# An mLSTM with two mixtures of dense layers: state in one 64x64 plane, gates partly on GpSimd, a lag between two blocks, and a new order

## The chip, the cores and the metric

The kernel runs on one core of a Trainium2 chip. The metric is the device time of one execution in microseconds (us). The engines of the core are named as the profile names them: PE is TensorE (matmuls; PEld is its weight load), DVE is VectorE, ACT is ScalarE, POOL is GpSimd, SP issues all the DMAs. POOL works on SBUF alone, PE writes PSUM alone, and PSUM has eight banks of 512 fp32 columns here.

## The reference

Three layers follow each other. The first is a recurrent one: 2 batches of 8 heads, 768 steps, head size 40. The other two are dense layers over the 1536 tokens.

```python
for t in range(S):                       # per head: state C (40x40), n (40), m
    m_new = max(f[t] + m, i[t]);  f_s = exp(f[t] + m - m_new);  i_s = exp(i[t] - m_new)
    C = f_s * C + i_s * outer(v[t], k[t]);   n = f_s * n + i_s * k[t]
    y[t] = sigmoid(o[t]) * (C @ q[t]) / max(abs(n @ q[t]), 1)
h = y @ w_in;  g = P(h) / (Q(abs(h)) + 1e-6);  x = g @ w_out        # 320 -> 2048 -> 320
xn = x / rms(x) * rms_g;  out = (silu(xn @ w_gate) * (xn @ w_val)) @ w_out2   # 320 -> 1536 -> 320
```

## The kernel before

**Stages.** The recurrent layer is cut into 12 chunks of 128 steps (6 for each batch, numbered j). In a chunk the steps are done as matrix products: `s` (keys times queries, L504), `f` (forget gates spread over the partitions, L484), `scan` (their running products, L487), `a` (product of the two, L509), `y` (times the values, L537). What earlier chunks left comes from the state tile `cst`: `yi` multiplies it with the queries (L527), `ys` scales that and takes it out of PSUM (L531), and `u` (L549), `cd` (L555) and `ca` (L563, L565) bring the state up to date. Then come the denominator, the output gate and a transpose (`xt`, L645) into `xall`.

The first dense layer works on pairs (block of 256 tokens, 256 of the 2048 columns): 48 pairs, each with 16 matmuls in (L676), a chain of some ten elementwise operations on ACT, DVE and POOL (L709 to L749), and matmuls out (L681, or L695 and L697). `PAIRS` lists them: blocks 0 and 1 in turn over the eight column groups, then blocks 2 to 5. The weights arrive as 64-bit words that DVE, ACT and POOL turn into fp32 halves (`weight`, L304 to L392). The second dense layer (L846 to L960) has its matmuls at L865 and L873 to L875.

**The gates.** One tile holds the gates of all 16 heads on 16 partitions. They are worked in two parts, steps 0 to 255 and 256 to 767: running maximum (L423), sums (L430, L431 on DVE, L434 on POOL), exponential (L437), forget factors in fp16 (L441), running products in a chunk (`gate_d`, L449), transposes (L455). No chunk can start its `f` before L441 of its part.

**The state.** `cst` is 128 partitions by 4 pairs of heads by 2 by 41. Even heads stand on partitions 0 to 39 in plane 0, odd heads on 64 to 103 in plane 1, and the rest is kept zero, so that one matmul over 128 partitions gives both heads of a pair. POOL clears that rest once (L409, L410).

**What sets the order.** Nothing is scheduled on the chip or by the compiler: every step is a task, `ORDER` is a list of 1948 task numbers, and each engine gets its instructions in the sequence in which the tasks stand there. Tiles and PSUM banks are taken from rings (`ring("b", banks)` for the eight banks) when a task starts and given back when another ends, so the list also decides which bank each task writes and what it has to wait for. `yi` takes one bank (L615), `ys` gives it back.

Of the kernel before, what the change touches and what calls it, by code (L numbers as in the profile page):

```python
# [121 lines left out]
def kernel(  # L122
# [148 lines left out]
    for nm, n in (("k", 2), ("v", 2)):
        ring("l" + nm, tiles(at, n, [128, H, D], FP32, "l" + nm))
    qk_bufs = tiles(at, 2, [128, 2, HP, L], FP32, "lqk")
    ring("lqk", qk_bufs)
# [827 lines left out]
```

## Time and profile before

| | us |
|---|---|
| median of 3 runs (481.05 to 481.11) | 481.09 |
| the profiled execution's own time | 481.12 |
| its span, first to last instruction | 479.3 |
| PE busy | 456.4 |
| DVE busy | 331.1 |
| POOL busy | 317.5 |
| ACT busy | 304.8 |

The profile is of one execution. Its span is 1.8 us shorter than its time, which is what lies around the first and the last instruction. Busy times are shares of the span: PE has hardly a gap, the three elementwise engines are about two thirds busy, but in stretches: the 40 slices of the page show DVE at 8 or more from the second slice to the 25th, and ACT from the fifth, with one 7, to the 24th.

### The profile page before, as it was taken

How to read it: one execution, taken by the hardware profiler on the slowest of the kernel's cores; microseconds unless marked ns; L12 is line 12 of the kernel's file. 1: busy time of each engine (PE TensorE's matmuls, PEld its weight loads, DVE VectorE, ACT ScalarE, POOL GpSimd, SP SyncE). 2: the span in 40 equal slices, each digit the busy share in tenths (PEclk: the TensorE clock that was granted, in tenths of full speed). 3: DMA queues.
4: the chain of work that ended last, by engine and by line, in shares of the span. 5: the costliest groups of instructions: out<-in, count | busy, mean ns of one | idle time of the engine just before them, and what ended most of it. 6: DMA issues, size and time to landing. Idle time of an engine off the chain costs nothing.

```text
span 479.3 us, 9356 instructions
## 1 busy us (share of the span) xinstructions
PE 456.4 (95%) x3552; PEld 414.5 (86%) x3552; DVE 331.1 (69%) x609; ACT 304.8 (64%) x576; POOL 317.5 (66%) x337
## 2 busy tenths in 40 slices
PE   3699899989999999999999999999999999999996
PEld 2588778778789999999999988888898889999996
DVE  7999999999999989899999999875210210201211
ACT  3245999999998899799999988552422212212311
POOL 5689999999998898886977778990831303213320
PEclk9998999999999999999999999999999999999999
DMA  8869371325032060010322144571100000000001
GB/s 239 273 204 255 101 196 31 114 61 143 1 102 63 1 203 3 1 42 2 115 90 83 38 160 166 180 233 59 34 15 27 1 0 2 1 27 29 1 14 57
DMA packets 18366, 40.41 MB, mean 84 GB/s; under 512 B 3952, under 2 KB 11904, under 8 KB 18320
## 3 DMA queue, kind: packets, MB, share of 16 engines
q1 hardware_dynamic: 18320, 39.80, 27.4%
q8 instruction: 28, 0.46, 0.4%
q14 instruction: 18, 0.15, 0.1%
HBM read 35.86 MB, written 3.93 MB: 83 GB/s over the span
## 4 chain that ended last, share of the span: by engine, by line
PE 65%; ACT 14%; POOL 9%; DVE 8%; issue 3%; DMA 1%; POOLq 0%; DVEq 0%; ACTq 0%
PE bank L865 26%; PE bank L676 10%; PE bank L695 5%; PE bank L875 4%; PE bank L873 4%; PE bank L874 4%; PE bank L681 4%; POOL z L720 2%; PE bank L697 2%; ACT z L710 2%; ACT u L709 2%; ACT bank L732 2%; ACT vv L718 1%; DVE w_buf L487 1%; POOL cv L356 1%
## 5 line engine op out<-in xcount | busy, mean ns | idle before, releaser
L676 PE MATMUL bank<-xall,win 128*128 128x256 f32 x768 | 104.0, 289 | 3.5 <-ACT yb L543 1.6
L676 PEld LDWEIGHTS bank<-xall,win 128*128 128x128 f32 x768 | 96.5, 193 | 7.1 <-ACT yb L543 1.8
L941 DVE TENSOR_TENSOR vv<-bank,vv 128x512 f32<-128x512 f32 x35 | 23.6, 688 | 98.0 <-PE bank L865 97.8
L720 POOL TENSOR_TENSOR z<-z,u 128x512 f32<-128x512 f32 x48 | 62.0, 1292 | 14.1 <-ACT z L710 13.1
L947 POOL TENSOR_TENSOR wou<-vv,wou 128x512 fp32r<-128x512 f32 x16 | 20.7, 1295 | 53.7 <-ACT wou L944 49.4
L938 ACT ACTIVATE vv<-bank 128x512 f32<-128x512 f32 x35 | 20.7, 595 | 50.6 <-PE bank L865 46.2
L865 PE MATMUL bank<-xall,w2gv 128*128 128x512 f32 (+1 forms) x256 | 46.4, 337 | 0.0
L749 POOL TENSOR_TENSOR gl<-vv,gh 128x512 fp32r<-128x512 f32 x32 | 41.3, 1296 | 5.6 <-ACT gh L748 3.8
L865 PEld LDWEIGHTS bank<-xall,w2gv 128*128 128x128 f32 x256 | 39.2, 190 | 4.7 <-DVE vv L739 0.2
L710 ACT ACTIVATE z<-u,few 128x512 f32<-128x512 f32 x48 | 39.2, 816 | 1.0
L695 PE MATMUL bank<-wou,gh 128*128 128x320 f32 x128 | 38.9, 316 | 0.0
L697 PE MATMUL bank<-wou,gh 128*128 128x320 f32 x128 | 38.0, 309 | 0.0
L681 PE MATMUL bank<-scr,vv 128*128 128x320 f32 x128 | 37.1, 435 | 0.0
L737 DVE SCALAR_TENSOR_TENSOR bank<-vv,few,bank 128x512 f32<-128x512 f32 x48 | 35.8, 749 | 0.0
L735 DVE SCALAR_TENSOR_TENSOR z<-z,bank 128x512 f32<-128x512 f32 x48 | 32.6, 682 | 4.4 <-ACT bank L734 3.6
L732 ACT ACTIVATE bank<-z,few 128x512 f32<-128x512 f32 x48 | 32.9, 686 | 2.5 <-DVE vv L729 2.5
L739 DVE SCALAR_TENSOR_TENSOR vv<-z,bank 128x512 f32<-128x512 f32 x48 | 32.6, 683 | 0.6
L331 DVE TENSOR_SCALAR bank<-raw 128x320 int32<-128x320 int32 x68 | 32.6, 486 | 0.3
L709 ACT ACTIVATE u<-bank 128x512 f32<-128x512 f32 x48 | 28.7, 598 | 4.0 <-POOL z L720 1.8
L865 PE MATMUL bank<-win,w2gv 128*128 128x512 f32 x128 | 31.1, 391 | 0.0
L681 PEld LDWEIGHTS bank<-scr,vv 128*128 128x128 f32 x128 | 23.2, 190 | 8.2 <-DVE vv L739 0.2
L364 POOL TENSOR_TENSOR win<-cv,win 64x128 fp32r<-64x128 f32 (+2 forms) x37 | 28.0, 757 | 2.4 <-ACT win L360 0.5
(169 smaller groups left out, 1180.3 us busy)
## 6 DMA issues: line engine op xcount, KB each, us to landing
raw<-in_w_out_dram SPq DMA_DIRECT2D x14, 640.0 KB, 4.1
raw<-in_w_gv_dram SPq DMA_DIRECT2D x12, 640.0 KB, 4.3
raw<-in_w_in_dram SPq DMA_DIRECT2D x8, 640.0 KB, 5.8
lqk<-in_qk_tr_dram SPq DMA_DIRECT2D x24, 192.0 KB, 4.7
los<-in_o_gate_dram SPq DMA_DIRECT2D x12, 160.0 KB, 3.6
lv<-in_v_dram SPq DMA_DIRECT2D x12, 160.0 KB, 4.3
lk<-in_k_dram SPq DMA_DIRECT2D x12, 160.0 KB, 3.8
z_dram<-rnd SPq DMA_DIRECT2D x6, 320.0 KB, 4.8
```

Of the source, the lines that this page charges most:

```text
L331: DVE.tensor_scalar(out=mid(x), in0=word(x, 1), scalar1=3, scalar2=0x3FFFFFFF, op0=ALU.logical_shift_left, op1=ALU.bitwise_and,)
L676: PE.matmul(out=hb()[:, e], lhsT=l, rhs=r, start=(x == 0), stop=(x == len(mm) - 1))
L681: PE.matmul(out=T("acc", n, t)[:, 0:DM], lhsT=T("vv", i)[:, e, t * 128:(t + 1) * 128], rhs=w[:, e], start=p + e == 0, stop=p == NPAIR - 1 ...
L695: PE.matmul(out=o, lhsT=l, rhs=woh[:, e], start=first, stop=last)
L697: PE.matmul(out=o, lhsT=l, rhs=wol[:, e], start=False, stop=False)
L709: go("hu", lambda: ACT.activation(out=u(), in_=hb(), func=ACTF.Abs), [("in1", i)], ["u"])
L710: go("z", lambda: ACT.activation(out=z(), in_=u(), func=ACTF.Identity, scale=babs[:, 1:2], bias=babs[:, 0:1]), [("hu", i)], ["z"])
L720: go("zu", lambda: POOL.tensor_tensor(out=z(), in0=z(), in1=u(), op=ALU.mult), [("z", i)], [], ["u"])
L732: go("ars", lambda: ACT.activation(out=hb(), in_=z(), func=ACTF.Abs_reciprocal_sqrt, bias=cq), [("zu", i), ("p3", i)])
L737: go("y2", lambda: DVE.scalar_tensor_tensor(out=hb(), in0=vv(), scalar=nacoef[:, 0:1], in1=hb(), op0=ALU.add, op1=ALU.mult), [("w", i)])
L749: go("gl", lambda: POOL.tensor_tensor(out=gl(), in0=vv(), in1=r32(gh()), op=ALU.subtract), [("gh", i)], ["gl"], ["vv"])
L865: PE.matmul(out=bank(i, e), lhsT=l, rhs=r, start=y == 0, stop=y == len(mm) - 1)
```

## The change

Five edits, and a new order.

- The state loses its planes: `cst` is 128 by 4 by 41, odd heads stand below even ones in one plane. `yi` therefore multiplies each head by itself, in tiles of 64 partitions by 64 columns (16 calls of 41 columns in place of 8 of 82), and writes even and odd heads to two banks; `ys` becomes two operations of 164 columns. `cd` and `ca` become one operation each over all 128 partitions instead of two over 40.
- `u` loads 64 columns of keys instead of 40 (the next head's first 24 come along) and so writes all 128 partitions; the key tiles get 24 columns of zeros at their end (L411 of the changed kernel). The memsets of `lqk` and `cst` go.
- The three sums of the gates all run on one engine: DVE for the first part, POOL for the second.
- The running products of the gates take their zero from a word of a PSUM bank, where it was an SBUF tile.
- `LAG = 1`: the pairs of block 1 run one column group behind those of block 0.
- `ORDER` is another list throughout.

```diff
-    PAIRS = [(n, p) for p in range(NPAIR) for n in range(2)] + [(n, p) for n in range(2, NB) for p in range(NPAIR)]
+    PAIRS = [(n, x - n * LAG) for x in range(NPAIR + LAG) for n in range(2) if 0 <= x - n * LAG < NPAIR]
+    PAIRS += [(n, p) for n in range(2, NB) for p in range(NPAIR)]
...
-    cst = at.tile([128, HP, 2, D1], FP32, name="cst")
+    cst = at.tile([128, HP, D1], FP32, name="cst")
...
-        for t in qk_bufs:
-            for r0 in (32, 96):
-                POOL.memset(t[r0:r0 + 32, 0], 0.0)
-        POOL.memset(cst, 0.0)
+        for t in lk_bufs:
+            POOL.memset(t[:, H * D:], 0.0)
...
     def gate_a(a, b):
-        gf = gate_in[:, 0, a:b]
-        DVE.tensor_tensor(out=gf, in0=gf, in1=m_t[:, a:b], op=ALU.add)
-        DVE.tensor_tensor(out=g48[FR, a:b], in0=gf, in1=m_t[:, a + 1:b + 1], op=ALU.subtract)
-
-    def gate_i(a, b):
-        POOL.tensor_tensor(out=g48[0:BH, a:b], in0=gate_in[:, 1, a:b], in1=m_t[:, a + 1:b + 1], op=ALU.subtract)
+        e = POOL if a else DVE
+        gf, m1 = gate_in[:, 0, a:b], m_t[:, a + 1:b + 1]
+        e.tensor_tensor(out=gf, in0=gf, in1=m_t[:, a:b], op=ALU.add)
+        e.tensor_tensor(out=g48[FR, a:b], in0=gf, in1=m1, op=ALU.subtract)
+        e.tensor_tensor(out=g48[0:BH, a:b], in0=gate_in[:, 1, a:b], in1=m1, op=ALU.subtract)
...
     def gate_d(a, b):
+        zc = T("gt", a)[FR, 511:512]
+        DVE.memset(zc, 0.0)
...
-            DVE.tensor_tensor_scan(out=sl, data0=sl, data1=zc[FR].to_broadcast([BH, L]), initial=1.0, op0=ALU.mult, op1=ALU.add)
+            DVE.tensor_tensor_scan(out=sl, data0=sl, data1=zc.to_broadcast([BH, L]), initial=1.0, op0=ALU.mult, op1=ALU.add)
...
         def yi():
-            t = heads("pi")
             for p in range(HP):
                 for c in (slice(0, 64), slice(64, 128)):
-                    PE.matmul(out=t[c, 2 * p:2 * p + 2], lhsT=T("lqk", j)[:, 0, p, c], rhs=cst[:, p])
+                    for e in range(2):
+                        r = slice(64 * e, 64 * e + D)
+                        PE.matmul(out=odd(e)[c, p], lhsT=T("lqk", j)[r, 0, p, c], rhs=cst[r, p])
...
         def ys():
-            dd = idt[:, ch, 32 + b * H:32 + (b + 1) * H][:, :, None].to_broadcast([128, H, D1])
-            DVE.tensor_tensor(out=T("yb", j), in0=heads("pi"), in1=dd, op=ALU.mult)
+            dd = idt[:, ch, 32 + b * H:32 + (b + 1) * H].rearrange("p (a e) -> p a e", e=2)
+            for e in range(2):
+                DVE.tensor_tensor(
+                    out=T("yb", j).rearrange("p (a e) d -> p a e d", e=2)[:, :, e], in0=odd(e),
+                    in1=dd[:, :, e:e + 1].to_broadcast([128, HP, D1]), op=ALU.mult,
+                )
...
-                PE.matmul(out=t[r0:r0 + D, h // 2], lhsT=T("lk", j)[:, h], rhs=v2_buf[:, h])
+                PE.matmul(out=t[r0:r0 + 64, h // 2], lhsT=T("lk", j)[:, h * D:h * D + 64], rhs=v2_buf[:, h])
...
         def cd():
-            for e in range(2):
-                r = slice(64 * e, 64 * e + D)
-                dd = dl[r, ch, b * HP:(b + 1) * HP][:, :, None].to_broadcast([D, HP, D1])
-                POOL.tensor_tensor(out=cst[r, :, e, 0:D1], in0=cst[r, :, e, 0:D1], in1=dd, op=ALU.mult)
+            dd = dl[:, ch, b * HP:(b + 1) * HP][:, :, None].to_broadcast([128, HP, D1])
+            POOL.tensor_tensor(out=cst, in0=cst, in1=dd, op=ALU.mult)
...
-            for e in range(2):
-                r = slice(64 * e, 64 * e + D)
-                cc = cst[r, :, e, 0:D1]
-                if ch:
-                    DVE.tensor_tensor(out=cc, in0=t[r], in1=cc, op=ALU.add)
-                else:
-                    DVE.tensor_copy(out=cc, in_=t[r])
+            if ch:
+                DVE.tensor_tensor(out=cst, in0=t, in1=cst, op=ALU.add)
+            else:
+                DVE.tensor_copy(out=cst, in_=t)
...
-            task(("yi", j), yi, [("s", j), ("ca", j - 1)], take=[key_(("pi", j))], give=[("lqk", j)])
-            task(("ys", j), ys, [("yi", j), ("gates", ch)], take=[("yb", ("yb", j))], give=[("pi", j)])
+            task(("yi", j), yi, [("s", j), ("ca", j - 1)], take=[key_(("pi", j, e)) for e in range(2)],
+                 give=[("lqk", j)])
+            task(("ys", j), ys, [("yi", j), ("gates", ch)], take=[("yb", ("yb", j))],
+                 give=[("pi", j, e) for e in range(2)])
```

Of the order, whose numbers tell a reader nothing, one line of the list of before and one of the change:

```diff
-    0, 8, 19, 9, 374, 10, 21, 375, 376, 377, 3, 20, 36, 11, 2, 12, 13, 22, 23, 39, 26, 378, 15, 24, 41, 42, 45, 46, 1,
+    0, 8, 9, 18, 10, 34, 3, 2, 11, 14, 12, 39, 1, 40, 43, 41, 391, 396, 392, 44, 394, 393, 13, 60, 19, 37, 20, 21, 24,
```

How the order stands on three engines, a row for each instruction or run of equal ones (source line, operation, destination and source tile, shape):

DVE from the first running maximum of the gates (L423, L424 of the change) on, before:

```order
L423 SCALAR_TENSOR_TENSOR scr<-scr 16x256
L423 SCALAR_TENSOR_TENSOR scr<-scr 16x512
L430 TENSOR_TENSOR scr<-scr 16x256
L431 TENSOR_TENSOR scr<-scr 16x256
L430 TENSOR_TENSOR scr<-scr 16x512
L431 TENSOR_TENSOR scr<-scr 16x512
L331 TENSOR_SCALAR bank_69<-raw_83 128x320
L337 SCALAR_TENSOR_TENSOR cv_88<-raw_83,bank_69 128x320
L331 TENSOR_SCALAR bank_70<-raw_83 128x320
L441 SCALAR_TENSOR_TENSOR f_112<-scr,f_112 16x256
L444 MEMSET f_112 48x2
L449 SCALAR_TENSOR_TENSOR scr<-scr,zc 16x128 x2
```

and in the change:

```order
L424 SCALAR_TENSOR_TENSOR scr<-scr 16x256
L432 TENSOR_TENSOR scr<-scr 16x256
L433 TENSOR_TENSOR scr<-scr 16x256
L434 TENSOR_TENSOR scr<-scr 16x256
L424 SCALAR_TENSOR_TENSOR scr<-scr 16x512
L441 SCALAR_TENSOR_TENSOR f_112<-scr,f_112 16x256
L444 MEMSET f_112 48x2
L448 MEMSET bank_69 16x1
L451 SCALAR_TENSOR_TENSOR scr<-scr,bank_69 16x128 x2
L489 SCALAR_TENSOR_TENSOR w_buf<-bank_72,id_106 128x512
```

The sums of the first part move ahead of the second part's maximum, the second part's leave DVE, and the first chunk's scan (L489) stands right behind the running products, ahead of all weight conversion.

POOL from its first memset of the program on, before:

```order
L402 MEMSET f_112 48x768
L406 MEMSET zc 48x1
L409 MEMSET lqk_124 32x512 x2
L409 MEMSET lqk_125 32x512 x2
L410 MEMSET cst 128x328
L434 ISA
L434 TENSOR_TENSOR scr<-scr 16x256
L434 TENSOR_TENSOR scr<-scr 16x512
L356 TENSOR_TENSOR cv_88<-cv_88,rnd_86 128x640
```

and in the change:

```order
L406 MEMSET f_112 48x768
L411 MEMSET lk_121 128x24
L411 MEMSET lk_122 128x24
L432 ISA
L432 TENSOR_TENSOR scr<-scr 16x512
L433 TENSOR_TENSOR scr<-scr 16x512
L434 TENSOR_TENSOR scr<-scr 16x512
L360 TENSOR_TENSOR cv_88<-cv_88,rnd_86 128x640
```

Four large memsets and one sum of 256 columns go, two sums of 512 columns come.

PE around the first matmuls of a pair (L676, L683 of the change), before; L527 is `yi`:

```order
L537 MATMUL bank_70<-vp_buf,scr 64x41 x16
L676 MATMUL bank_69<-xall,win 128x256 x16
L645 MATMUL bank_70<-ident,los 128x128 x3
L549 MATMUL bank_72<-v_buf,lk_121 40x41 x8
L645 MATMUL bank_76<-ident,los 128x128 x3
...
L527 MATMUL bank_70<-cst,lqk_124 64x82 x8
L676 MATMUL bank_76<-xall,win 128x256 x16
```

and in the change, where `yi` is L530:

```order
L559 MATMUL bank_69<-v_buf,lk_121 64x41 x8
L652 MATMUL bank_70<-ident,los 128x128 x3
L530 MATMUL bank_73<-cst,lqk_123 64x41
L530 MATMUL bank_71<-cst,lqk_123 64x41
...
L547 MATMUL bank_76<-vp_buf,scr 64x41 x16
L683 MATMUL bank_73<-xall,win 128x256 x16
L506 MATMUL bank_74<-lqk_123 128x128
```

The first pair stood behind `s` and `f` of chunk 4 and `y` of chunk 3; it now stands behind `y` of chunk 2, ahead of `s` of chunk 4. `yi` alternates between two banks.

## Rows read from the trace of the kernel before

**Rows 1.** Windows by stage: length, busy us (count) per engine, PE clock, DMA

```profile
core 0: us, PE busy (x) PEld busy (x) DVE busy (x) ACT busy (x) POOL busy (x), PEclk, DMA share, GB/s
0.00:48.00 48.00, 34.47 (x374) 29.77 (x374) 43.98 (x87) 19.54 (x40) 35.85 (x58) 0.96 0.83 242
48.00:104.00 56.00, 50.75 (x460) 42.38 (x460) 53.32 (x96) 53.76 (x95) 54.02 (x59) 1.00 0.36 106
104.00:220.00 116.00, 116.00 (x1069) 105.13 (x1069) 108.79 (x185) 104.94 (x201) 103.50 (x110) 1.00 0.20 59
220.00:284.00 64.00, 63.54 (x467) 59.90 (x466) 61.75 (x115) 62.96 (x119) 49.62 (x46) 1.00 0.25 76
284.00:479.30 195.30, 191.60 (x1189) 177.27 (x1187) 63.29 (x130) 63.59 (x125) 74.53 (x68) 1.00 0.17 57
```

**Rows 2.** Chain of waits, in order of time: start us, length us, what

```profile
10.61 0.73 DVE scr L449 x2
12.72 2.65 DVE scr L449 x4
58.64 1.30 POOL z L720
103.77 2.17 PE bank L676 x16
```

**Rows 3.** Waits of PE, 48 to 104 us: total, times, longest

```profile
PE bank L676 <- ACT yb L543: 1.6, 1, 1.6
PE bank L676 <- DVE yb L531: 0.6, 1, 0.6
```

**Rows 4.** Groups of DVE by shape: busy us, mean ns, idle before

```profile
L563 DVE TENSOR_TENSOR cst<-bank,cst 40x164 f32<-40x164 f32 x16 | 5.2, 322 | 0.8 <-PE bank L549 0.6
L531 DVE TENSOR_TENSOR yb<-bank,idt 128x328 f32<-128x328 f32 x10 | 4.9, 491 | 0.7 <-PE bank L527 0.6
L431 DVE TENSOR_TENSOR scr<-scr 16x256 f32<-16x256 f32 x1 | 1.2, 1196 | 0.0
L430 DVE TENSOR_TENSOR scr<-scr 16x256 f32<-16x256 f32 x1 | 0.8, 782 | 0.0
L431 DVE TENSOR_TENSOR scr<-scr 16x512 f32<-16x512 f32 x1 | 0.7, 682 | 0.0
L441 DVE SCALAR_TENSOR_TENSOR f<-scr,f 16x256 f16<-16x256 f32 x1 | 0.4, 414 | 0.0
```

**Rows 5.** Windows of L563, L565, L531 (DVE) and L549 (PE, PEld)

```profile
0.00:104.00 104.00, 2.57 (x8) 0.98 0.57 169
...
0.00:104.00 104.00, 0.63 (x2) 0.98 0.57 169
...
0.00:104.00 104.00, 2.45 (x5) 0.98 0.57 169
...
104.00:220.00 116.00, 2.53 (x80) 1.94 (x80) 1.00 0.20 59
```

**Rows 6.** Groups of POOL by shape

```profile
L555 POOL TENSOR_TENSOR cst<-cst,dl 40x164 f32<-40x164 f32 x16 | 7.4, 460 | 0.6
L409 POOL MEMSET lqk<- 32x512 f32 x4 | 2.1, 518 | 0.2
L434 POOL TENSOR_TENSOR scr<-scr 16x256 f32<-16x256 f32 x1 | 1.5, 1485 | 0.0
L434 POOL TENSOR_TENSOR scr<-scr 16x512 f32<-16x512 f32 x1 | 1.3, 1261 | 0.0
```

**Rows 7.** Timeline of PE: start us, length us, line, shapes, records

```profile
44.90 3.16 PE L676 MATMUL bank<-xall,win 128*128 128x256 f32 x16
...
154.04 1.13 PE L537 MATMUL bank<-vp_buf,scr 128*64 128x41 f32 x32
...
169.86 0.79 PE L527 MATMUL bank<-cst,lqk 128*64 128x82 f32 x16
...
189.92 0.51 PE L549 MATMUL bank<-v_buf,lk 128*40 128x41 f32 x16
```

**Rows 8.** Group of PE by shape: busy us, mean ns

```profile
L537 PE MATMUL bank<-vp_buf,scr 128*64 128x41 f32 x384 | 16.5, 254 | 1.8 <-DVE xall L653 1.1 <-DVE scr L509 0.6
```

**Rows 9.** Timeline of POOL, 12 to 16 us: the operation beside the four scans

```profile
12.83 1.63 POOL L356 TENSOR_TENSOR cv<-cv,rnd 128x640 int32<-128x640 int32 x1 [5.86 <-DVE cv L337]
```

More of the change, by code (lines that the diff above doesn't have):

```diff
@@ L22 @@
 NATIVE = [0, 1, 2, 3, 4, 5, 6, 7, 8, 9, 10, 11, 12, 13, 14, 15]
+LAG = 1
 BY_SQUARE = [0, 2, 4, 6, 8, 10, 12, 14, 16, 18, 20, 22, 24, 26, 28]
 ORDER = [
[93 rows of a table removed]
[93 rows of a table added]
 ]
@@ L267 @@
     dl = at.tile([128, NCH, BH // 2], FP32, name="dl")
-    cst = at.tile([128, HP, 2, D1], FP32, name="cst")
-    zc = at.tile([48, 1], FP32, name="zc")
+    cst = at.tile([128, HP, D1], FP32, name="cst")
     den = at.tile([128, H, 1], FP32, name="den")
[L271 to L274, printed above, removed]
+    ring("lv", tiles(at, 2, [128, H, D], FP32, "lv"))
+    lk_bufs = tiles(at, 2, [128, H * D + 64 - D], FP32, "lk")
+    ring("lk", lk_bufs)
+    ring("lqk", tiles(at, 2, [128, 2, HP, L], FP32, "lqk"))
     ring("yb", tiles(at, 2, [128, H, D1], FP32, "yb"))
@@ L284, in load @@
             src = {"k": k, "v": v, "o": o_gate}[nm][i * L:(i + 1) * L].rearrange("p (h d) -> p h d", h=H)
-            nc.sync.dma_start(out=lo_of(i) if nm == "o" else T("l" + nm, i), in_=src)
+            dst = lo_of(i) if nm == "o" else T("l" + nm, i)
+            if nm == "k":
+                dst = dst[:, 0:H * D].rearrange("p (h d) -> p h d", h=H)
+            nc.sync.dma_start(out=dst, in_=src)
             return
@@ L405, in setup @@
         DVE.memset(eps6, 1e-6)
-        POOL.memset(zc, 0.0)
-        for t in qk_bufs:
-            for r0 in (32, 96):
-                POOL.memset(t[r0:r0 + 32, 0], 0.0)
-        POOL.memset(cst, 0.0)
+        for t in lk_bufs:
+            POOL.memset(t[:, H * D:], 0.0)
         for nm, dst, src in (
@@ L523, in yi, with odd @@
         def yi():
-            t = heads("pi")
             for p in range(HP):
                 for c in (slice(0, 64), slice(64, 128)):
-                    PE.matmul(out=t[c, 2 * p:2 * p + 2], lhsT=T("lqk", j)[:, 0, p, c], rhs=cst[:, p])
-        def ys():
-            dd = idt[:, ch, 32 + b * H:32 + (b + 1) * H][:, :, None].to_broadcast([128, H, D1])
-            DVE.tensor_tensor(out=T("yb", j), in0=heads("pi"), in1=dd, op=ALU.mult)
+                    for e in range(2):
+                        r = slice(64 * e, 64 * e + D)
+                        PE.matmul(out=odd(e)[c, p], lhsT=T("lqk", j)[r, 0, p, c], rhs=cst[r, p])
+        def odd(e):
+            return T("pi", j, e)[:, 0:HP * D1].rearrange("p (a b) -> p a b", a=HP)
+        def ys():
+            dd = idt[:, ch, 32 + b * H:32 + (b + 1) * H].rearrange("p (a e) -> p a e", e=2)
[4 more added lines that the diff above has]
+                )
         def y():
@@ L986 @@
                [("ld", "gates")] + ([("gm", parts[x - 1][0])] if x else []))
-            go("gi", lambda a=a, b=b: gate_i(a, b), [("gm", a)])
             go("ga", lambda a=a, b=b: gate_a(a, b), [("gm", a)])
-            go("gb", lambda a=a, b=b: gate_b(a, b), [("ga", a), ("gi", a)])
+            go("gb", lambda a=a, b=b: gate_b(a, b), [("ga", a)])
             go("gc", lambda a=a, b=b: gate_c(a, b), [("gb", a)])
-            go("gd", lambda a=a, b=b: gate_d(a, b), [("gc", a)])
-            go("ge", lambda a=a, b=b: gate_e(a, b), [("gd", a), ("ld", "eye")], take=[("b", ("gt", a))],
-               give=[("gt", a)])
+            go("gd", lambda a=a, b=b: gate_d(a, b), [("gc", a)], take=[("b", ("gt", a))])
+            go("ge", lambda a=a, b=b: gate_e(a, b), [("gd", a), ("ld", "eye")], give=[("gt", a)])
             for c in range(a // L, b // L):
```

184 rows, old and new, of the table ORDER are left out of this document.

## The prediction

> **What bounds the kernel now.** I first read the busy time of each engine by stage [rows 1], cut where the chain of waits changes. From 104 us to 284 us PE is busy 179.5 of 180 us, and from there to the end 191.6 of 195.3 us. So from 104 us on PE is the bound, and the time is the moment at which PE becomes full, plus the work it then has left. Before that, PE idles: it is busy 34.5 of the first 48 us, and its first sixteen matmuls of a pair take 3.16 us where sixteen later take 2.17 [rows 2, 7]; the granted clock is 0.96 on average there and 1.00 afterwards [rows 1]. What PE waits for in that head is read from the others. DVE is busy 44.0 of 48 us and then 53.3 of 56 us; ACT only 19.5 of the first 48, then 53.8 of 56; POOL 35.9, then 54.0 of 56 [rows 1]. So until 48 us it is DVE that sets the pace, and from 48 to 104 us DVE, ACT and POOL together, each at 95% or more. The chain says the same: gate scans on DVE at 10.6 and 12.7 us, a POOL product at 58.6 us, and from 103.8 us PE [rows 2]. The last thing that made PE wait long was a bank: 1.6 us for the evacuation by L543, and before that 0.6 us for `ys` [rows 3]. From all this the rule for the change: work taken off DVE before 104 us moves the end by as much, if ACT and POOL do not hold it back; work added on PE counts where it comes after 104 us.
>
> **DVE before 104 us.** `ca` runs for five chunks there, ten instructions [rows 5], at 0.32 us each [rows 4]; five remain. They go over 128 partitions instead of 40, but over the same 164 columns, so I keep 0.32: -1.6 us. `ys` runs five times there [rows 5] at 0.49 us for 328 columns; two halves of 164 columns cost between 0.25 each (half of it: 0) and 0.49 each (+2.45 us). The nearest row is `ca`, 164 columns from PSUM at 0.32: 5 x (0.64 - 0.49) = +0.75 us. The sums of the gates' second part go to POOL: two of 0.68 us, -1.36 us. Those of the first part took 0.78 and 1.20 us while POOL ran its own two sums beside them; an operation of 256 columns that ran alone took 0.41 [rows 4]. Three of these make 1.23 us in place of 1.98: -0.75 us; if they were stretched like the worst one, 3.6 us, it would be +1.6, but POOL has only small memsets left to do there. The running products: two that ran alone took 0.73 us, four took 2.65 us [rows 2] while a POOL addition of 1.63 us ran beside them [rows 9]; alone the four would have taken 1.46. Their zero now comes from PSUM, so one SBUF input is left: -1.19 us if that ends the stretch, 0 if not. I take the first, since the two that ran alone, with both operands in SBUF, show that nothing but the neighbour stretched the four. Against this, L441 of the first part now runs beside the three POOL sums. The one such case in the trace cost 1.20 - 0.41 = 0.79 us [rows 4], so +0.79. The sum is -3.36 us.
>
> What that last term rests on has a rule in the Trainium skill. The page "SBUF — State Buffer", section "SBUF: two separate sides", says that a VectorE operation with two SBUF inputs and a GpSimd operation lock each other out for a whole instruction. By it L441 could wait one full POOL sum, 1.26 us [rows 6], and the gain would be 0.47 us smaller; the 1.19 us that four scans lost beside one POOL operation [rows 2, 9] agree with it.
>
> **POOL and ACT before 104 us.** POOL loses four memsets of 0.52, two sums of 1.49 and 1.26 and half of eight `cd` of 0.46, and gains three sums of 1.26 [rows 6]: -4.8 - 1.8 + 3.8 = -2.8 us beside DVE's -3.36. ACT yields nothing; but it is busy only 19.5 of the first 48 us [rows 1], and the new order puts the first pair's matmuls behind `y` of chunk 2, where they stood behind `y` of chunk 3, so that its share can begin sooner. That is why I let the whole 3.36 us through.
>
> **PE after 104 us.** `u` runs for five chunks there, 80 records [rows 5]. With 64 columns of weights it has the shape of `y`, whose 32 records take 1.13 us with 0.25 us for the last one [rows 7, 8]: 16 records take 15/31 x 0.88 + 0.25 = 0.68 us in place of 0.51, +0.17 each, +0.85 us. `yi` of chunks 7 to 11 goes from 16 records and 0.79 us [rows 7] to 32 records of `y`'s length. If two tiles work at a time, as the trace shows for `y`, that is 1.13 us, +0.34 each, +1.7 us. If four do, half of 0.88 and 0.25, 0.69 us: -0.10 each, -0.5 us. I take four: `s`, split by rows, and `y`, split by columns, have each half of the array to themselves, and the new tiles only combine the two. So PE gets +0.35 us, at worst +2.55.
>
> The Trainium skill's "TensorEngine Tiling (Array Packing)", section "Key Properties", has tiles load weights and multiply independently of each other, which makes 64x64 tiles four at a time. By it the term is -0.5 us, by the two at a time that the rows of `y` allow +1.7; no run here shows four.
>
> **Banks.** `yi` holds two of eight banks, and the second comes free only after the second half of `ys`, 0.15 us later than now. PE waited once for that bank, 0.6 us [rows 3]. I put 0.3 us for two such delays; the ends are 0 and a rival below.
>
> **Sum.** The profiled execution took 481.12 us (span 479.3 and 1.8 around it), the median of the runs is 481.09. 481.12 - 3.36 + 0.35 + 0.3 = 478.4 us.
>
> **Rivals.** *ACT holds the head.* ACT's work is the same, it is as full as DVE from 48 us on [rows 1], and if its first pair does not begin sooner, what DVE saves is idle time: 481.12 + 0.35 + 0.3 = 481.8 us. Against it: ACT has 28 us free before 48 us. *The small tiles run two at a time.* Then the change does not do on PE what it says: 478.4 + 2.2 = 480.6 us. For it: all rows show pairs. *Banks run out.* While blocks 0 and 1 interleave, four of eight banks hold their sums, and after 104 us five `yi` each need two at once. PE waits for the first matmul of a pair as in [rows 3], 1.6 and 0.6 us, 1.1 us on average and 0.15 us for the later return: 5 x 1.25 = 6.25 us in place of 0.3, 484.4 us. It makes the kernel slower once the five waits exceed 0.8 us each. Against it: after 104 us, PE's gaps are hardly there, and blocks 2 to 5 hold two banks instead of four. *The new list also closes DVE's idle time.* From 48 to 104 us DVE idles 56 - 53.3 = 2.7 us; a list made for the lighter chain could win that too: 475.7 us. Against it: it is spread over many short waits.
>
> **How the numbers follow.** My forecast has 0.47 (its own range 476.8 to 480.1), ACT 0.13, tiles by two 0.09, banks 0.17, idle time closed 0.14. About 0.2%, 1 us, is what a measurement of this kernel can tell from no change. Faster are the forecast and the last: 0.61. The same are ACT and the tiles: 0.22. Slower are the banks: 0.17. The range 474.6 to 482.6 leaves out most of the banks' case, whose waits would have to stay small, and the edge of the last one.
>
> **What would show it.** Right: PE full before 101 us, DVE busy time lower by about 3 us in the head, the six scans of the gates near 0.37 us each, `u` near 0.68 us and `yi` near 0.69 us when the clock is full, POOL lower by some 5 us in all. Wrong: PE full no sooner than 104 us though DVE has less to do, `yi` at 1.1 us, or PE waits of 0.5 us and more in front of pairs that follow `yi` or `ys`. Most of all I would be wrong if the new list puts a pair's chain behind a chunk's where the old one had it ahead; that changes PE's idle time by whole operations of 0.7 us, in either direction, and the sums above do not see it.

## The result, and the profile after

| | time, us (median; lowest to highest) | ratio to before, 95% interval |
|---|---|---|
| before | 481.12 (481.05 to 481.15, 7 runs) | |
| changed | 484.68 (484.13 to 488.24, 7 runs) | 1.0089 (1.0064 to 1.0114) |
| predicted | 478.4, range 474.6 to 482.6 | |

The kernel became 3.6 us slower, where I had put 2.7 us faster. The profiled execution shown here took 484.65 us (span 482.8). The windows of the changed kernel, with the columns and cuts of [rows 1]:

```profile
0.00:48.00 48.00, 35.64 (x426) 31.16 (x426) 39.65 (x88) 23.23 (x46) 33.98 (x53) 1.00 0.81 245
48.00:104.00 56.00, 52.57 (x460) 43.11 (x458) 51.38 (x92) 48.46 (x84) 52.13 (x55) 0.97 0.41 127
104.00:220.00 116.00, 113.66 (x1162) 103.28 (x1161) 107.52 (x183) 105.71 (x197) 100.31 (x106) 1.00 0.17 48
220.00:284.00 64.00, 61.93 (x460) 58.80 (x459) 61.22 (x117) 60.83 (x120) 48.17 (x45) 1.00 0.24 75
284.00:482.80 198.80, 195.45 (x1212) 180.78 (x1210) 65.32 (x134) 67.50 (x131) 77.74 (x70) 1.00 0.17 56
```

DVE's busy time in the first 104 us fell from 97.3 to 91.0 us, but its idle time rose by as much: 6.7 us before, 13.0 after. ACT, which idled 2.2 us from 48 to 104 us, idles 7.5. And PE, which was busy 179.5 of 180 us from 104 to 284 us, misses 4.4 us there.

The pieces themselves came out as worked out, nearly all of them. DVE's timeline of the gates in the changed kernel (start us, length us, line, operation): the three sums of the first part take 0.41 us each, the products on the chain 0.73 and 1.36 instead of 0.73 and 2.65 [rows 2], and the first scan of a chunk (L489) starts at 8.26 us.

```profile
4.72 0.41 DVE L433 TENSOR_TENSOR scr<-scr 16x256 f32<-16x256 f32 x1
5.16 0.41 DVE L434 TENSOR_TENSOR scr<-scr 16x256 f32<-16x256 f32 x1
...
6.80 0.41 DVE L441 SCALAR_TENSOR_TENSOR f<-scr,f 16x256 f16<-16x256 f32 x1
...
8.26 1.22 DVE L489 TENSOR_TENSOR_SCAN w_buf<-bank,id 128x512 f32<-128x512 f32 x1
...
13.58 1.36 DVE L451 TENSOR_TENSOR_SCAN scr<-scr,bank 16x128 f32<-16x128 f32 x4
```

The four products at 13.58 us still have a neighbour on POOL, an addition of the same kind as before [rows 9], and are no longer stretched:

```profile
13.59 1.53 POOL L360 TENSOR_TENSOR cv<-cv,rnd 128x640 int32<-128x640 int32 x1 [2.92 <-ACT rnd L354]
```

So where did the time go? I made one number per moment out of PE's records, an estimate: the elapsed time, less the time that the matmuls issued so far would take at the full clock (for each kind the median distance to the next start after 120 us). It is roughly the time that PE has lost until then, by idling or by the lower clock. Differences between two kernels are what the one lost more; they are good to some tenths of a us, since they depend on how each kind of matmul is priced. The kernels e1 to e11 are the experiments below; each column is its profiled execution.

| at us | before | changed | e1: changed code, old list | e4: gates only, old list | e7: three `den` moved | e11: four `den` moved |
|---|---|---|---|---|---|---|
| 20 | 15.9 | 14.7 | 15.1 | 15.3 | 14.6 | 14.9 |
| 40 | 26.0 | 26.3 | 24.4 | 25.3 | 26.3 | 25.3 |
| 50 | 30.7 | 28.8 | 28.7 | 30.1 | 28.8 | 27.7 |
| 60 | 31.7 | 33.1 | 30.1 | 30.9 | 32.3 | 30.5 |
| 110 | 37.7 | 39.3 | 35.5 | 35.9 | 36.1 | 34.0 |
| 220 | 42.6 | 44.5 | 41.4 | 41.1 | 41.3 | 39.3 |
| 300 | 45.7 | 49.3 | 44.4 | 44.1 | 45.5 | 43.5 |
| end | 46.4 | 49.9 | 45.2 | 44.9 | 46.2 | 44.0 |

The changed kernel is 1.9 us ahead of before at 50 us, and 1.4 us behind at 60. It loses 1.7 us more between 220 and 300 us. In front of these losses stand waits in a `den` chain, one of them at 22 us. The denominator of a chunk goes from ACT (absolute value) to POOL (maximum, L576), to DVE (reciprocal, L578) and back to POOL (`rs`, L582), and each step waits in the queue of its engine. POOL from 25 to 28 us, and DVE from 22 us on and at 49 us:

```profile
25.39 0.72 POOL L582 TENSOR_TENSOR los<-los,den 128x320 f32<-128x320 f32 x1 [2.92 <-DVE den L578]
...
27.25 0.75 POOL L517 TENSOR_TENSOR v_buf<-vp_buf,w_buf 128x328 f32<-128x328 f32 x1
```

```profile
22.65 1.22 DVE L489 TENSOR_TENSOR_SCAN w_buf<-bank,id 128x512 f32<-128x512 f32 x1
23.91 1.29 DVE L511 TENSOR_TENSOR scr<-bank,w_buf 128x512 f32<-128x512 f32 x2
25.12 0.19 DVE L578 RECIPROCAL den<-den 128x8 f32<-128x8 f32 x1
...
28.03 2.34 DVE L489 TENSOR_TENSOR_SCAN w_buf<-bank,id 128x512 f32<-128x512 f32 x2 [2.29 <-POOL v_buf L517]
...
48.98 1.22 DVE L489 TENSOR_TENSOR_SCAN w_buf<-bank,id 128x512 f32<-128x512 f32 x1
50.11 0.18 DVE L578 RECIPROCAL den<-den 128x8 f32<-128x8 f32 x1
```

The reciprocal of chunk 0 takes 0.19 us, but stands behind a scan and two products of chunk 1. POOL stands 2.92 us for it, with `v2` of chunk 1 (L517) queued behind, and the scan of chunk 2 waits 2.29 us for that. At 49 us the reciprocal of chunk 3 stands behind a scan of 1.22 us; in PE's timeline what follows from it is the 1.48 us ahead of the second transposes:

```profile
50.07 0.49 PE L652 MATMUL bank<-ident,los 128*128 128x128 f32 x3
52.04 0.63 PE L652 MATMUL bank<-ident,los 128*128 128x128 f32 x3 [1.48 <-POOL los L585]
...
53.84 5.45 PE L683 MATMUL bank<-xall,win 128*128 128x256 f32 x31 [0.21 <-DVE xall L660]
...
61.28 1.22 PE L683 MATMUL bank<-xall,win 128*128 128x256 f32 x8 [0.45 <-DVE vv L746]
...
105.65 1.13 PE L547 MATMUL bank<-vp_buf,scr 128*64 128x41 f32 x32 [1.32 <-DVE scr L341]
107.55 2.17 PE L683 MATMUL bank<-xall,win 128*128 128x256 f32 x16 [0.76 <-DVE vv L746]
...
228.73 0.42 PE L702 MATMUL bank<-wou,gh 128*128 128x320 f32 x1 [1.05 <-DVE vv L746]
```

Later it goes the other way: the reciprocal stands too early, DVE stands still for POOL's maximum, and a weight conversion (L341, whose bank `y` needs) and a pair's chain (L744, L746) wait behind it. These are the waits in front of the last three rows of PE:

```profile
104.39 0.20 DVE L578 RECIPROCAL den<-den 128x8 f32<-128x8 f32 x1 [2.59 <-POOL den L576]
...
226.47 0.20 DVE L578 RECIPROCAL den<-den 128x8 f32<-128x8 f32 x1 [1.45 <-POOL den L576]
```

These waits came with the list. From 18 to 290 us POOL stands 11.3 us in all for DVE's reciprocals in the changed kernel, and DVE 5.6 us for POOL's maximum. The same code in the old list (e1) has 1.6 us of the first, and none of the second. The first line is the changed kernel's, the second e1's (total, times, longest):

```profile
POOL los L582 <- DVE den L578: 11.3, 8, 2.9
...
POOL los L582 <- DVE den L578: 1.6, 2, 1.0
```

### The profile page after: what moved, and what is told of

It is laid out like the page before. It is cut to its first block, busy times and chain, and to the rows that moved or that the text cites. A ratio compares the mean times of both kernels' runs of the same rounds, so it can differ in the third digit from the quotient of the medians.

```text
span 482.8 us, 9655 instructions
## 1 busy us (share of the span) xinstructions
PE 459.2 (95%) x3712; PEld 417.1 (86%) x3712; DVE 325.1 (67%) x610; ACT 305.7 (63%) x576; POOL 312.3 (65%) x326
## 4 chain that ended last, share of the span: by engine, by line
PE 70%; ACT 10%; POOL 7%; DVE 7%; issue 3%; DMA 1%; SPq 1%; POOLq 0%; DVEq 0%
PE bank L872 27%; PE bank L683 13%; PE bank L702 5%; PE bank L882 4%; PE bank L881 4%; PE bank L880 4%; PE bank L688 3%; PE bank L704 2%; PE bank L547 2%; ACT bank L739 1%; DVE w_buf L489 1%; ACT z L717 1%; PE bank L652 1%; POOL z L727 1%; ACT bank L741 1%
## 5 line engine op out<-in xcount | busy, mean ns | idle before, releaser
L683 PE MATMUL bank<-xall,win 128*128 128x256 f32 x768 | 106.5, 293 | 3.2 <-DVE vv L746 1.4
L683 PEld LDWEIGHTS bank<-xall,win 128*128 128x128 f32 x768 | 98.5, 196 | 7.7 <-DVE xall L660 2.2
L872 PE MATMUL bank<-xall,w2gv 128*128 128x512 f32 (+1 forms) x256 | 46.4, 337 | 0.1
L954 POOL TENSOR_TENSOR wou<-vv,wou 128x512 fp32r<-128x512 f32 x17 | 22.0, 1298 | 36.1 <-ACT wou L951 33.9
L872 PEld LDWEIGHTS bank<-xall,w2gv 128*128 128x128 f32 x256 | 39.3, 190 | 5.2 <-ACT vv L945 0.3
L744 DVE SCALAR_TENSOR_TENSOR bank<-vv,few,bank 128x512 f32<-128x512 f32 x48 | 35.8, 747 | 0.0
L746 DVE SCALAR_TENSOR_TENSOR vv<-z,bank 128x512 f32<-128x512 f32 x48 | 32.6, 682 | 0.6
L489 DVE TENSOR_TENSOR_SCAN w_buf<-bank,id 128x512 f32<-128x512 f32 x24 | 29.0, 1216 | 3.3 <-POOL v_buf L517 2.3
```

What stands on the lines that cost most here:

```text
L489: DVE.tensor_tensor_scan(out=w_buf[:, 4 * g:4 * g + 4].rearrange("p a b -> p (a b)"), data0=T("pf", j, g), data1=id4, initial=0.0, op0=ALU ...
L683: PE.matmul(out=hb()[:, e], lhsT=l, rhs=r, start=(x == 0), stop=(x == len(mm) - 1))
L744: go("y2", lambda: DVE.scalar_tensor_tensor(out=hb(), in0=vv(), scalar=nacoef[:, 0:1], in1=hb(), op0=ALU.add, op1=ALU.mult), [("w", i)])
L872: PE.matmul(out=bank(i, e), lhsT=l, rhs=r, start=y == 0, stop=y == len(mm) - 1)
```

## The experiments

Twelve kernels. A ratio is to the kernel before, run again beside each, with its 95% interval.

**e1: the changed code in the old list.** The list and the lock-step pairs of before; `yi` and `ys` of chunk 4 had to stand behind `xl` of chunk 3, since `yi` takes two banks.

```diff
-LAG = 1
+LAG = 0
-ORDER = [ 0, 8, 9, 18, 10, 34, ...
+ORDER = [ the list of before, without gi ]
```

> The changed code (state plane of 64x64 tiles, half of the gates on GpSimd, zero in PSUM), issued in the order of the kernel before: its list and its lock-step pairs. Two places differ from the old list, since yi of chunk 4 needs two banks: it stands behind xl of chunk 3, and ys of chunk 4 right behind it. Theory 1 (the list costs the time, the edits pay what I summed, 2.7 to 2.9 us): 478 to 479.5 us. Theory 2 (the edits themselves cost the time, on PE or by the second bank): 483 to 485 us. Theory 3 (the edits only turn DVE's work into idle time, the list costs the 3.6 us): 480.7 to 482 us.

Measured: 480.94 us, ratio 0.9999 (0.9990 to 1.0007), runs from 479.96 to 482.94. The new list costs 3.7 us against the old one with the same code, and the edits together bring nothing in the median. That is the third theory's range, but not its reason: e4 and e10 show a gain of 1.3 us and a loss of 0.7 us in it. In its profiled execution (479.96 us, the fastest of its runs) PE leads by 2.2 us at 110 us and by 1.2 at the end. Among PE's waits from 40 to 160 us (total, times, longest) are those for the second bank of `yi`: the L530 row, 0.46 and 0.35 us, and 0.58 us of the row above it.

```profile
PE bank L683 <- DVE yb L538: 1.3, 2, 0.7
PE bank L530 <- DVE xall L660: 0.8, 2, 0.5
```

**e2: the old code in the new list.**

```diff
-    PAIRS = [(n, p) for p in range(NPAIR) for n in range(2)] + ...
+    PAIRS = [(n, x - n * LAG) for x in range(NPAIR + LAG) for n in range(2) if 0 <= x - n * LAG < NPAIR]
+ORDER = [ the list of after, with gi right ahead of ga ]
```

> The code of the kernel before, issued in the changed kernel's list with its pairs of the second block one behind; POOL's two sums of the gates stand right ahead of ga. Theory 1 (the list costs, the edits pay): the list's loss without the edits' gain, 486 to 488 us. Theory 2 (the edits cost the time): about the time before, 480.5 to 482 us. Theory 3 (edits worth nothing, list costs 3.6): 484 to 485.5 us.

Measured: 496.15 us, ratio 1.0317 (1.0303 to 1.0331). None of the theories had this: the old code is 15 us slower in the new list, so list and code don't add. The new list puts the gates' second part late, which on DVE delays chunks 2 on; PE waits 5.0 us in all for its products. That is the largest of its waits, and not the whole 15 us:

```profile
PE bank L457 <- DVE scr L451: 5.0, 3, 3.3
```

**e3: `v2` ahead of `rs` on POOL.** In the new list, POOL's rows in the head:

```diff
-L582 TENSOR_TENSOR los<-los,den 128x320
-L585 TENSOR_TENSOR los<-yb_125,los 128x320
-L586 COPY los<-los 128x64
 L517 TENSOR_TENSOR v_buf<-vp_buf,w_buf 128x328
...
 L563 TENSOR_TENSOR cst<-cst,dl 128x164
+L582 TENSOR_TENSOR los<-los,den 128x320
+L585 TENSOR_TENSOR los<-yb_125,los 128x320
+L586 COPY los<-los 128x64
```

> The changed kernel with one move in its list: rs, xm and xt of chunk 0 stand behind v2 and cd of chunk 1, as they did before, so POOL no longer waits 2.9 us for den of chunk 0 with v2 of chunk 1 behind it. Theory 1 with this place as the list's main loss: DVE's wait of 2.29 us for v2 goes, 482 to 483 us against the changed kernel's 484.7. If the loss lies in the stretches after 50 us (half clock over the first dense pairs, waits of 0.5 to 1.5 us at 105, 228 and 262 us): 484 to 485 us, although the wait goes.

Measured: 486.54 us, ratio 1.0111 (1.0087 to 1.0135); fastest run 484.61. DVE's wait for `v2` went, and another took its place, as DVE's timeline shows: with `xm` of chunk 0 later, PE's transposes of chunk 0 came late, and `y` of chunk 1 stands behind them in PE's queue.

```profile
26.08 2.33 DVE L489 TENSOR_TENSOR_SCAN w_buf<-bank,id 128x512 f32<-128x512 f32 x2
...
32.45 0.50 DVE L551 TENSOR_TENSOR yb<-bank,yb 128x328 f32<-128x328 f32 x1 [2.87 <-PE bank L547]
```

Moving the waiting instruction back only moved the wait; the late reciprocal was the cause (e11).

**e4: the gates' part alone, in the old list.** The code of before with `gate_a` on POOL for the second part, the zero in PSUM, no `gate_i`:

```diff
-        gf = gate_in[:, 0, a:b]
-        DVE.tensor_tensor(out=gf, in0=gf, in1=m_t[:, a:b], op=ALU.add)
+        e = POOL if a else DVE
+        e.tensor_tensor(out=gf, in0=gf, in1=m_t[:, a:b], op=ALU.add)
...
+        zc = T("gt", a)[FR, 511:512]
+        DVE.memset(zc, 0.0)
```

> The kernel before with only the gates' part of the change (second part's three sums on POOL, first part's three on DVE, zero of the running product in PSUM), in the old list without gi. My sum for these terms was -2.5 us. Theory 1: 478.4 to 479.5 us. Theories 2 and 3: 480.7 to 481.5 us, since what DVE saves before 16 us is idle later (theory 2 would then put all the loss on the state plane).

Measured: 479.80 us, ratio 0.9972 (0.9962 to 0.9983), runs from 479.58 to 479.94. Faster by 1.3 us, half of my 2.5, and between the theories. DVE's and POOL's rows show why: in this list POOL's sums start between DVE's, and DVE's take 0.39, 1.37 and 1.21 us, 2.97 in all, the upper bound of my term and not its 1.23.

```profile
5.09 0.39 DVE L429 TENSOR_TENSOR scr<-scr 16x256 f32<-16x256 f32 x1
5.51 1.37 DVE L430 TENSOR_TENSOR scr<-scr 16x256 f32<-16x256 f32 x1
6.89 1.21 DVE L431 TENSOR_TENSOR scr<-scr 16x256 f32<-16x256 f32 x1
```

```profile
5.24 1.35 POOL L429 TENSOR_TENSOR scr<-scr 16x512 f32<-16x512 f32 x1 [1.06 <-DVE scr L421]
```

With 2.97 the terms are -1.36 + (2.97 - 1.98) + (1.36 - 2.65) = -1.7 us, near the 1.8 by which PE leads at 110 us and the 1.5 at the end. What DVE saves early does come through to the end in the old list: from the second on, each of the 48 pairs starts 1.5 to 1.6 us sooner than before.

**e5: `den` of chunk 3 ahead of the scan.** In the new list, DVE's rows:

```diff
 L341 SCALAR_TENSOR_TENSOR scr<-raw_84,bank_69 128x320
+L578 RECIPROCAL den<-den 128x8
 L489 SCALAR_TENSOR_TENSOR w_buf<-bank_71,id_106 128x512
-L578 RECIPROCAL den<-den 128x8
```

> The changed kernel with one row of its list moved: the reciprocal den of chunk 3 stands ahead of the scan of chunk 4 on DVE, not behind it (1.22 us). Theory A (in the new list the denominators' chain, which crosses ACT, POOL and DVE, stands at the wrong places, and PE pays for it): rs and xm of chunk 3 start 1.1 us sooner, PE's wait of 1.48 us at 50.6 us shrinks to 0.4, and if the half clock at 54.2 us comes from that pause it goes as well, 1.7 us more: 482 to 483.6 us. Theory B (the loss is in the clock alone, and in work of PE that the list can't move): 484 to 485 us.

Measured: 484.97 us, ratio 1.0080 (1.0063 to 1.0098); the fastest run 483.56 against the changed kernel's 484.13. By the medians it gave nothing. In the profiled execution PE's wait at 50 us shrank from 1.48 to 0.41 us, the clock stayed full from 42.6 us on, and PE ended 1.0 us sooner. My 1.7 us for the clock were wrong, as PE's timeline says: pair 4 still waits for DVE's chain of the pairs before it, and starts 0.95 us sooner than the 61.28 shown above, not 2.7.

```profile
51.09 0.63 PE L652 MATMUL bank<-ident,los 128*128 128x128 f32 x3 [0.41 <-POOL los L585]
...
53.38 3.97 PE L683 MATMUL bank<-xall,win 128*128 128x256 f32 x31 [0.21 <-DVE xall L660]
...
60.33 1.21 PE L683 MATMUL bank<-xall,win 128*128 128x256 f32 x8 [1.44 <-DVE vv L746]
```

So this reciprocal is only part of what is lost between 50 and 60 us. There the changed kernel loses 4.3 us by the table, before 1.0, e7 3.5 and e11 2.8. What the rest is, no run here shows.

**e6: `den` of chunks 5 and 11 later.** DVE's rows, twice of this kind:

```diff
-L578 RECIPROCAL den<-den 128x8
 L744 SCALAR_TENSOR_TENSOR bank_69<-vv_96,few,bank_69 128x512
 L341 SCALAR_TENSOR_TENSOR bank_76<-raw_84,bank_76 128x320
 L335 TENSOR_SCALAR bank_74<-raw_84 128x320
 L746 SCALAR_TENSOR_TENSOR vv_96<-z_92,bank_69 128x512
+L578 RECIPROCAL den<-den 128x8
```

> The changed kernel with two reciprocals moved back on DVE, behind the last operation of the next pair (den of chunk 5 behind g of pair 9, den of chunk 11 behind g of pair 34). Theory A: DVE no longer stands 2.6 us at 101.8 us and 1.45 us at 225 us with a conversion and a pair's chain queued behind it; PE's waits of 1.32 and 0.76 us at 105 to 107 us and of 1.05 us at 228.7 us go: 481.6 to 483 us. Theory B: PE is full there and what it saves is given back in other waits: 484 to 485 us.

Measured: 483.47 us, ratio 1.0057 (1.0038 to 1.0076); fastest 481.81 against 484.13. The median lies 0.5 us above what theory A allowed. The profiled execution is 1.7 us shorter than the changed kernel's. It ran 1.0 us late up to its twelfth pair, ahead of both moved instructions; from the thirteenth pair on, behind the reciprocal of chunk 5, it is 1.2 us early, a step of 2.2 us.

**e7: all three.**

```diff
 the moves of e5 and e6 together
```

> The changed kernel with all three reciprocals moved as in the two others. Theory A: the two gains add up, 479.5 to 482 us, near the 480.9 us that the same code took in the old list. Theory B: 484 to 485 us.

Measured: 482.28 us, ratio 1.0025 (1.0007 to 1.0042); fastest and profiled run 480.89. One of its twelve runs took 883.3 us, for a reason that the record does not show; without it the median is 482.15. The medians went down by 2.4 us, a little short of the expected, the profiled ones by 3.8. PE's waits from 100 to 290 us (total, times, longest): the first fence is e7's, the second the changed kernel's, of which one is left.

```profile
PE bank L683 <- DVE xall L660: 1.3, 3, 0.6
```

```profile
PE bank L547 <- DVE scr L341: 1.3, 1, 1.3
PE bank L683 <- DVE xall L660: 1.2, 3, 0.6
PE bank L702 <- DVE vv L746: 1.1, 1, 1.1
PE bank L683 <- DVE vv L746: 0.8, 1, 0.8
```

**e8: PE kept busy at 51 us.** In the changed kernel:

```diff
+            for _ in range(8 if j == 3 else 0):
+                PE.transpose(out=T("pt", j)[:, 384:512], in_=ident, identity=ident)
             to_t(los[:, j % NLO], T("pt", j))
```

> The changed kernel, with eight more 128x128 transposes of the identity (into columns that nobody reads) in PE's queue ahead of the transposes of chunk 3, where PE stands 1.48 us. They cost 0.9 us of that pause at most. If PE's pause there is what makes the granted clock fall to half for 3.4 us at 54.2 us: the fall goes, 1.7 us less, 482.5 to 483.5 us, and the runs lie closer together than 484.1 to 488.2. If the clock falls whatever PE does there: 484 to 485 us, spread as before.

Measured: 487.16 us, ratio 1.0120 (1.0105 to 1.0136), the opposite of what I hoped. In the profiled execution the clock no longer fell at 54 us, and fell at 61.4 and 109.2 us instead (windows: PE busy, PEld, DVE, ACT, POOL, then the granted clock):

```profile
61.40:64.80 3.40, 3.40 (x40) 3.18 (x42) 2.63 (x3) 3.35 (x6) 3.17 (x5) 0.50 0.00 0
...
109.20:112.60 3.40, 3.40 (x17) 3.40 (x17) 3.33 (x6) 1.27 (x2) 3.40 (x3) 0.50 0.00 0
```

And PE waited at 61.24 us for the same result of DVE (L751 here) as at 61.28 without the filling:

```profile
61.24 1.09 PE L688 MATMUL bank<-xall,win 128*128 128x256 f32 x4 [1.94 <-DVE vv L751]
```

So what e8 lost came behind 61 us, and in the profiled execution of the changed kernel the half clock from 54.2 to 57.7 us cost next to nothing: DVE was late anyway.

**e9: the changed code in the old list, `yi` of chunks 4 and 8 later.**

```diff
 PE's queue, e1 against this:
-yi(4) in0(1) in1(1)
+in0(1) in1(1) yi(4)
-yi(8) out0(17)
+out0(17) yi(8)
```

> The changed code in the old list, as in the run that took 480.9 us, with yi moved back at the two places where PE waited for its second bank: yi of chunk 4 behind the matmuls of pair 1 (waits of 0.46 and 0.58 us), yi of chunk 8 behind the first output product of pair 17 (0.35 us). If the second bank is what the state plane costs beside its 0.3 us of matmul work: 479.6 to 480.3 us. If the rest of what the head gained is lost elsewhere: 480.6 to 481.3 us.

Measured: 479.49 us, ratio 0.9965 (0.9953 to 0.9978), runs from 479.25 to 479.78. Against e1 that is 1.45 us by the medians, 0.7 by the fastest runs and 0.2 by the profiled executions; the rest is that its runs lie closer together. In that execution most of the waits are still there, ahead of L683: 1.1 us for `ys` (L538), where e1 had 1.3, and 0.7 us for `xall` (L660), where `yi` had waited 0.8. So that the second bank's waits made the difference is not shown.

**e10: the state plane alone, in the old list.**

```diff
 the changed code, with gate_a, gate_i and zc of before
```

> Only the state plane of 64x64 tiles (yi, ys, u, cd, ca and the padded k), with the gates of the kernel before and its list, yi and ys of chunk 4 moved as in the first run. My terms for it were -0.85 us on DVE, +0.35 on PE and +0.3 for banks: 480.9 us. By the runs so far (all edits 480.9, gates alone 479.8) it costs: 481.5 to 482.5 us if the two parts add, 480.5 to 481.2 if they hinder each other.

Measured: 481.84 us, ratio 1.0025 (1.0014 to 1.0035). The state plane costs 0.7 us, where my three terms made -0.2. With the gates' -1.3 that is -0.6, and e1 showed -0.1: roughly a sum.

**e11: a fourth `den`.** e7, and DVE's rows in the head:

```diff
 L468 COPY dl<-bank_74 128x48
+L578 RECIPROCAL den<-den 128x8
 L489 SCALAR_TENSOR_TENSOR w_buf<-bank_75,id_106 128x512
 L511 TENSOR_TENSOR scr<-bank_76,w_buf 128x512
 L511 TENSOR_TENSOR scr<-bank_72,w_buf 128x512
-L578 RECIPROCAL den<-den 128x8
```

> The changed kernel with the three reciprocals moved (482.3 us) and a fourth: den of chunk 0 ahead of the scan of chunk 1 on DVE, where it waits for nothing, in place of behind that scan and two products of chunk 1. POOL's wait of 2.9 us at 22.5 us, with v2 of chunk 1 queued behind it, shrinks to about 0.5. If that wait is what the new list loses against the old one between 20 and 40 us (1.9 us of PE's work): 480 to 481 us. If DVE or ACT take its place: 482 to 483 us.

Measured: 479.60 us, ratio 0.9971 (0.9953 to 0.9990), fastest run 478.36. The four reciprocals are the only instructions whose place on an engine differs from the changed kernel's, 0.2 us of work each, and they are worth 5.1 us by the medians and 5.8 by the fastest runs: more than the whole loss. Where each one pays can be read from the starts of the 48 pairs, one profiled execution against the other. The reciprocal of chunk 0 brings 1.6 to 2.1 us from the first pair to the last (e11 against e7), that of chunk 3 some 1.0 us from the fifth pair on (e5 against the changed kernel). That of chunk 5 brings 2.2 us from the thirteenth (e6, e7), and that of chunk 11 1.3 us at the 39th, of which 0.5 is left at the last. POOL's wait in the head is down from 2.92 us:

```profile
23.35 0.72 POOL L582 TENSOR_TENSOR los<-los,den 128x320 f32<-128x320 f32 x1 [0.24 <-DVE den L578]
```

**e12: one more, on POOL.** e11, with POOL's maximum of chunk 2 ahead of `cd`, `vp` and a weight addition:

```diff
+L576 TENSOR_SCALAR den<-den 128x8
 L563 TENSOR_TENSOR cst<-cst,dl 128x164
 L496 TENSOR_TENSOR vp_buf<-lv_120,idt 128x8x40
 L499 COPY vp_buf<-idt 128x8
 L360 TENSOR_TENSOR cv_89<-cv_89,rnd_87 128x640
-L576 TENSOR_SCALAR den<-den 128x8
```

> The version with four reciprocals moved (479.6 us, 478.4 in its fastest runs) and one more move: POOL's maximum den1 of chunk 2 stands ahead of cd, vp and a weight addition, so that DVE no longer waits 1.2 us for it with the products a of chunk 3 behind it. If a wait of the denominators' chain in the head costs its own length at the end, as the first four did: 477.5 to 479 us. If ACT or the transposes of chunk 3 take its place: 479 to 480 us.

Measured: 479.15 us, ratio 0.9971 (0.9954 to 0.9987), fastest run 478.18: 0.2 us less than e11 by the fastest runs, and the intervals can't part the two. From 18 to 110 us DVE's wait for POOL's maximum fell from 1.5 to 0.3 us, but DVE now waits 1.1 us for PE (L486): another wait took its place. By the medians e9, e11 and e12 beat the kernel before by 1.5 to 1.9 us, and the changed one by 5.1 to 5.5.

## Why the prediction was wrong

**The step that failed** is the one that has no term. The sum prices every edit, and closes with "That is why I let the whole 3.36 us through": it takes the new list as neutral, apart from the first pair's place. The list is worth +3.7 us with the new code (e1 against the changed kernel), and moving four reciprocals in it gives back 5.1 us, more than all of it (e11). Runs at the same mean granted clock say the same: at 0.995 or 0.996 the changed kernel took 484.50 to 485.17 us (four runs), e1 480.88 to 481.46 (seven), e11 479.83 and 479.94. Whether moved reciprocals would have helped the old list too was not run; with 1.6 us of POOL's waits for them there, less is to be had. My last paragraph said that a list which puts one chain behind another "changes PE's idle time by whole operations of 0.7 us, in either direction, and the sums above do not see it". That was the right place, but I gave it no chance, no price and no rival. One of its signs came: PE is not full from 104 us on, though DVE has less to do. The order of DVE would have shown it: the reciprocal of chunk 3 behind a scan, that of chunk 5 ahead of a pair's L744 and L746.

**The rule** (work off DVE before 104 us moves the end by as much) holds in the old list within what I could measure: e4's terms, with the stretched sums, make -1.7, and 1.3 arrived by the medians, 1.5 by the profiled executions. In the new list it fails: DVE is busy 6.3 us less before 104 us, and it idles 6.3 us more. Of these the edits save some 4.7 by the measured sizes (`ca` 1.6, the gates' second part 1.4, first part 0.7, scans 1.3, less 0.3 for `ys`), where my sum had 3.4; the rest is put off.

**The terms on DVE.** Gates' second part to POOL and the scans with the zero in PSUM: right (1.29 us saved on the four scans, 1.19 put), with POOL's addition of 1.53 us still beside the scans. The first part's sums: 1.23 us as put in the new list, 2.97 in the old one. L441 was not stretched at all (0.79 put). `ca` and `ys`: groups of DVE in the changed kernel (busy us, mean ns) say 0.31 us each for `ca`, and ten pairs of halves of `ys` took 5.5 us, 0.55 a pair for the 0.64 I put [rows 4].

```profile
L538 DVE TENSOR_TENSOR yb<-bank,idt 128x164 f32<-128x164 f32 x20 | 5.5, 319 | 0.2
...
L568 DVE TENSOR_TENSOR cst<-bank,cst 128x164 f32<-128x164 f32 x8 | 2.5, 309 | 0.4 <-PE bank L559 0.4
...
L578 DVE RECIPROCAL den<-den 128x8 f32<-128x8 f32 x12 | 2.4, 196 | 5.6 <-POOL den L576 5.6
```

**PE.** Right: `u` took 0.67 us and `yi` 0.68 at the full clock, as the timeline shows at 48.4 and 52.6 us. The 32 records of `yi` start in fours, some 7 ns apart within a four, where those of `u` start in pairs. So four small tiles do work at a time, and that rival falls. The page "TensorEngine Tiling (Array Packing)" of the Trainium skill, section "Key Properties", had it right, for tiles of this size.

```profile
48.42 0.67 PE L559 MATMUL bank<-v_buf,lk 128*64 128x41 f32 x16
...
52.60 0.68 PE L530 MATMUL bank<-cst,lqk 40*64 40x41 f32 x32
```

What I read of the clock in the head was wrong: the 0.96 of [rows 1] for the first 48 us is no mean over them. The records of the clock begin at 40.3 us in that profile, and the time ahead of them counts as full (last section).

**Banks and the other rivals.** The banks' rival named 484.4 us, the time that came, but that is luck, since its mechanism isn't the cause: the changed kernel has no wait of PE at `yi` (in its waits L530 does not appear), so the new list gives it room. In the old list the second bank cost 1.4 us of waits (0.46, 0.58 and 0.35), where I had put 0.3; e9 took 0.7 us less by the fastest runs and 0.2 by the profiled executions. This term was too small by about 1.1 us there, which would explain why the state plane alone costs 0.7 us where my terms made -0.2 (e10). *ACT holds the head* falls: ACT idles 5.3 us more than before from 48 to 104 us. *The list closes DVE's idle time* went the other way: it rose from 2.7 to 4.6 us in that stretch.

## What to carry to other kernels

When a change comes with a new order, price the order as carefully as the edits: take each short instruction in the middle of a chain that crosses engines (here a reciprocal of 0.2 us), and look at what stands ahead of it on its engine and what is queued behind it on the engine that waits. Such an instruction can stand wrong in two ways: too late it holds the next engine (chunks 0 and 3), too early it blocks its own (chunks 5 and 11). Here it paid each time to move the short instruction itself: ahead of the long work that it stood behind, or behind the work that could have run in its wait. Moving the longer instructions that waited for it (e3) only moved the wait.
